# 24 attention items first in float32, then two token blocks per d_ff block

## Chip, cores, metric

One NeuronCore of a Trainium2 chip; all other cores are idle. The metric is the device time of one execution in microseconds (us), from the first to the last instruction and what lies around them.

## The reference

Sliding-window attention with a linear distance bias, then two MLPs on its output, all in float32:

```python
batch, n_heads, seq, head_dim = (4, 8, 576, 64);  n_tokens, d_model, d_ff = (2304, 512, 2048);  window = 128
...
    scores = scale * np.matmul(q, k.transpose(0, 1, 3, 2))
    mask = (rel >= 0) & (rel < window)
    scores = np.where(mask, scores + bias[None], -1000000000.0)
    scores = scores - np.max(scores, axis=-1, keepdims=True)
    attn = np.exp(scores)
    attn = attn / (np.sum(attn, axis=-1, keepdims=True) + 1e-09)
    return np.matmul(attn, v)
...
    h = x @ w_in;  g = np.maximum(h, 0.0) + alpha * np.minimum(h, 0.0);  x = g @ w_out         # first MLP
    h = x @ w_in2;  g = h * (1.0 / (1.0 + np.exp(-1.702 * h)));  out = g @ w_out2              # second MLP
```

The weights reach the kernel as 64-bit words and are turned into float32 on the chip.

## The kernel before, in words

**Attention items.** An item is one batch, one head and one unit of queries (`UNITS`: the first 256 queries, or the last 320). There are 64, in the order `u`, batch, head: 0 to 31 of the first unit, eight to a batch. An item runs through stages: load (`a_load`), scores on TensorE into a PSUM bank (`a_qk`), bias and row minimum on VectorE (`a_bias`, line 446), exponentials with row sums on ScalarE (`a_exp`, line 462), the sums plus 1e-9 and their reciprocal on VectorE (`a_recip`, lines 470 and 471), normalising on VectorE (`a_norm`, line 486), transposes on TensorE (`a_trans`, line 499), a copy of them to SBUF on ScalarE (`a_pt_hi`, line 506), the product with the values on TensorE (`a_av`), and for each pair of heads a high part and a rest of the result, on ScalarE and VectorE, into the ring `xh`/`xl` (`a_x3`, lines 572 and 573). The ring holds three blocks of 256 tokens.

**Two kinds of items.** The first `FP` = 16 are computed in float32: scores straight from the loaded rows (line 426, 64 rows), values placed into a zeroed tile by GpSimd (line 412), line 525 for the value product. All others are split into two float32r parts (`a_split`, lines 435, 436 and 537).

**Weights.** The first MLP has 32 chunks: for each d_ff block of 128 one of `w_in` and one of `w_out`, 512 KB each as it is loaded. A chunk is loaded (`w_load`, four buffers), then decoded: two operations on ScalarE (`w_scale`, lines 147 and 150), shift and add on VectorE (lines 154 and 159), and a split into a high part (line 107 on ScalarE; for chunks 0 and 2 line 108 on VectorE) and a rest (line 112 on VectorE). `w("...")` lets one chunk take one of these steps; while the list `pinned` isn't empty the decoding stays in its program order.

**Steps of the first MLP.** A step is one token block `k` and one d_ff block `f`: 12 matmuls for the hidden values (`m1_h`, line 586), a negated relu on ScalarE (line 600), the leaky combination on VectorE (line 606), its high part on ScalarE (line 608), the rest on VectorE, and two steps later (`LAG`) 12 matmuls into the block's accumulators (`m1_o`, line 632). After a block's last step ScalarE copies the accumulators and SP stores them (`x2d`, line 653). The steps run over all `f` of block 0, then all of block 1, then blocks 2 to 6 and a double block 7.

**Order.** Ten items (n = 0 to 9) are written out ahead of the steps, with decoding between their stages and idle matmuls (`busy`, counts in `WARM`) on TensorE. From item 10 on each step carries half an item (`item_a`: scores, transposes of the item ahead, bias, exponentials; `item_b`: value product, reciprocal, normalising), by the table `count` for the first 32 steps. At step 32 (`S2`) item 26 begins. In the first 32 steps each also moves one chunk on in its decoding, some of them two. Where nothing is pinned, the planner of the framework orders each engine's work by data dependences and its own estimate.

Of the kernel before, what the change touches and what calls it, by code (L numbers as in the profile page):

```python
# [43 lines left out]
HI_DVE = (0, 2)  # L44
NST, NWD = 4, 3
KM = NB1 - 2

FP = 16
# [6 lines left out]
WARM = (15, 3, 3, 2, 0, 1, 1, 1, 1, 1, 1)  # L55
# [14 lines left out]
def tile_window_attention__then__two_mlps(  # L70
# [248 lines left out]
    rawfs = [first.tile([P, UCOLS[0]], F32, name=f"rawf{i}") for i in range(2)]  # L319

    at = ExitStack()
    ps_a = at.enter_context(tc.tile_pool(name="ps_a", bufs=4, space=PSUM))
# [3 lines left out]
    sts = [ap_.tile([P, 16], F32, name=f"st{i}") for i in range(2)]  # L326
# [11 lines left out]
    pts = [apf.tile([P, 384], F32, name=f"pt{i}") for i in range(2)]  # L338
    zero = apf.tile([P, 512], BF16, name="zero")
# [79 lines left out]
    def a_qk(n, b, u, h, U):  # L419
        banks = [ps_a.tile([P, 2, 256], F32, tag="a", name="s") for _ in range(1 + u)]  # L420
# [20 lines left out]
    def a_bias(n, b, u, h, U):  # L441
        tt, s = tts[n % 2], sts[n % 2]
# [15 lines left out]
    def a_exp(n, b, u, h, U):  # L458
        tt, s = tts[n % 2], sts[n % 2]
# [7 lines left out]
    def a_recip(n, b, u, h, U):  # L467
        s = sts[n % 2]
# [4 lines left out]
    @stage  # L473
    def a_norm(n, b, u, h, U, eng):
        tt, s = tts[n % 2], sts[n % 2]
# [13 lines left out]
    def a_trans(n, b, u, h, U):  # L489
        tt = tts[n % 2]  # L490
        banks = [ps_a.tile([P, 512], F32, tag="a", name="pt") for _ in range(1 + u)]
# [10 lines left out]
    @stage  # L502
    def a_pt_hi(n, b, u, h, U, i):
        if i <= u:
            x, c, w = st["t", n][i]
            nc.scalar.copy(pts[n % 2] if n < FP else ar["pth"][:, c : c + w], x[:, :w])
# [13 lines left out]
    def a_av(n, b, u, h, U):  # L520
        if n < FP:
            x = st["x", n] = st["x", n - 1] if h % 2 else ps_a.tile([P, 512], F32, tag="a", name="x")
            pt, vz = pts[n % 2], vzs[n % 2]
# [7 lines left out]
        x = ps_a.tile([P, 512], F32, tag="a", name="x")  # L531
# [45 lines left out]
    gs, accs, part0 = {}, {}, []  # L577
# [39 lines left out]
    def m1_o(k, f):  # L617
# [4 lines left out]
        first = f == 0 or (k, f) == (0, 16)  # L622
        last = f == NF - 1 or (k, f) == (0, 16 - 1)
# [13 lines left out]
        if last:  # L637
            for i, a in enumerate(accs.pop(k)):
# [4 lines left out]
                if False:  # L643
                    pin(nc.vector.tensor_tensor(
                        xs, a, part0[0][:, i * DM : (i + 1) * DM].rearrange("p (i t) -> p i t", i=2), op=ALU.add
                    ))
                else:
                    copy("dve" if k == KM and i % 2 else "act", xs, a)
# [300 lines left out]
    idle = pso.tile([P, 2, T1], F32, tag="o1", name="idle")  # L949
# [4 lines left out]

    nc.vector.memset(zero, 0.0)
    for t in vzs:
# [3 lines left out]
    def w_first(n):  # L960
        for _ in range(n):
            i = wdone.get("load", 0)
            w_load(i)
            wdone["load"] = i + 1

    def bias_load(h, m):
        nc.sync.dma_start(out=relht[:, h : h + m, :], in_=relh[:, h : h + m, :])

    a_load(0, (0,))
# [8 lines left out]
    a_load(1, (1,))  # L978
    w_first(1)
    a_load(3, (0,))  # L980
    a_load(3, (1,))
    bias_load(4, 4)
    w_first(1)
    make_identity(nc, ident)
    busy(0)
    a_qk(0)
    w_ahead()
    def pre_load(n):
        if n + 4 < H + 2:
            a_load(n + 4)  # L990
        if n >= H:
            a_load(n + 2)

    def pre_qk(n):
        if n + 1 < H + 2:
            busy(n + 1)
            a_qk(n + 1)

    def pre_split(n):
        if n + 2 < H + 2:  # L1000
            a_split(n + 2)

    for n in range(H + 2):

        if n == 4:
# [4 lines left out]
            nc.gpsimd.tensor_scalar(beta, alph, -1.0, 1.0, op0=ALU.mult, op1=ALU.add)  # L1010
        a_av(n - 2)
        a_split_v(n)
        a_bias(n)
        w("split")
        a_exp(n)
        a_recip(n - 1)
        w("shift")
        a_norm(n - 1, "dve")
        a_trans(n - 1)
        w("add")  # L1020
        w_ahead()
        pre_load(n)
        a_x3(n - 2)
        a_pt_hi(n - 1, 0)
        a_pt_hi(n - 1, 1)
        pre_qk(n)
        w("scale")
        pre_split(n)
        if n in (0, 8, 9, 6, -1):
# [5 lines left out]
    n = H + 2  # L1035
    a_split(n)
    for i in range(2):
        a_pt_lo(n - 2, i)
    a_recip(n - 1)
    a_norm(n - 1, "dve")  # L1040
    a_av(n - 2)
    a_x1(n - 2)
    a_x2(n - 2)
    a_x3(n - 2)
# [4 lines left out]
    HF = 16  # L1049
    steps = [(0, f) for f in range(HF)] + [(1, f) for f in range(NF)] + [(0, f) for f in range(HF, NF)]  # L1050
# [3 lines left out]
    def item_a(n):  # L1054
        return (
            lambda: (a_trans(n - 1), a_qk(n), a_pt_hi(n - 1, 0)),
            lambda: (a_pt_hi(n - 1, 1), a_bias(n)),
            lambda: (a_pt_lo(n - 1, 0), a_pt_lo(n - 1, 1)),
# [4 lines left out]
    def item_b(n):  # L1063
        return (
            lambda: (
                a_av(n - 1), a_parts() if n == FP else None,
                a_recip(n), a_split_v(n), a_load(n + 2), a_norm(n, "dve"),
            ),
            lambda: a_x1(n - 1),
            lambda: a_x2(n - 1),  # L1070
            lambda: None,
            lambda: a_x3(n - 1),
# [3 lines left out]
    count = (1, 1, 1, 1, 1, 1, 1, 1, 1, 1, 1, 0, 1, 1, 2, 1, 1, 1, 1, 1, 1, 1, 1, 1, 1, 1, 1, 1, 2, 1, 1, 0)  # L1076
    halves, n = [], 2 * (H + 2)
    for c in count:
        halves.append([(item_a, item_b)[i % 2](i // 2) for i in range(n, n + c)])
        n += c  # L1080
    halves += [[(item_a, item_b)[i % 2](H + 2 + i // 2)] for i in range(S2, len(steps))]
    for s, (k, f) in enumerate(steps):
        n = H + 2 + s // 2
        if s == S2:
            pinned.clear()
        if (k, f) == (KM, 0):
            pinned.append(True)
        parts = halves[s]
        part = parts[0] if parts else NONE
        if len(parts) == 2:  # L1090
            m1_h(k, f)
            part[0]()
            part[1]()
            m1_n(k, f)
            m1_g(k, f)
            part[2]()
            part[3]()
            part[4]()
            w("shift")
            parts[1][0]()  # L1100
            parts[1][1]()
            w("add")
            w("scale")
            w_ahead()
            parts[1][2]()
            parts[1][3]()
            m1_lo(k, f, "dve")
            parts[1][4]()
# [279 lines left out]
```

## Time and profile before

| | us |
|---|---|
| median of 3 runs (lowest to highest) | 902.85 (900.74 to 903.24) |
| profiled execution, whole | 903.59 |
| its span, first to last instruction | 901.8 |
| TensorE busy | 885.6 (98%) |
| VectorE busy | 715.6 (79%) |
| ScalarE busy | 581.9 (65%) |
| GpSimd busy | 91.5 (10%) |

In the profile PE is TensorE, PEld its weight loads, DVE VectorE, ACT ScalarE, POOL GpSimd, SP the engine that issues the DMAs (SPq its queue). L586 is line 586 of the kernel. Matmuls are pipelined, and the duration of one includes a tail under which the next already runs: how long a row of matmuls takes is read from start to start. The same holds in a smaller measure for VectorE and ScalarE. A busy share is an average over stages with different limits.

### The profile page before, as it was taken

The page shows a single profiled execution, that of the slowest core. Times are in us where ns is not written, and L with a number is a line of the kernel's source. Part 1 is how long each engine was busy: PE and PEld are TensorE (multiplying, and loading weights), DVE is VectorE, ACT ScalarE, POOL GpSimd, SP SyncE. Part 2 cuts the span into 40 slices and gives each one's busy share as a digit, 9 for nine tenths or more (in the row PEclk, how much of TensorE's full clock was granted, in tenths as well). Part 3 has the DMA queues.
Part 4 walks back from the last instruction along what each step waited for, and adds up shares of the span by engine and source line. Part 5 has one row for each costly group of instructions (what it writes and reads, how often), then busy time and mean ns, then how long its engine had stood idle before and what let it go on. Part 6 is the DMA issues. An engine that isn't in the chain of part 4 may idle for free.

```text
span 901.8 us, 19339 instructions
## 1 busy us (share of the span) xinstructions
PE 885.6 (98%) x6882; PEld 848.9 (94%) x6884; DVE 715.6 (79%) x1906; ACT 581.9 (65%) x1459; POOL 91.5 (10%) x127
## 2 busy tenths in 40 slices
PE   7799999999999999999999999999999999999998
PEld 4589899999999999999988889999999999999998
DVE  5999877779989999999857777656665699989876
ACT  5999766767777778777645557655556755434332
POOL 1010111122222222222100000000000000000000
PEclk8989999999999999999999999999999999999999
DMA  8666521223424424235024324657668884544422
GB/s 256 213 210 210 166 80 48 83 81 99 163 87 124 132 87 143 84 89 163 19 72 139 94 74 162 206 190 242 237 237 286 286 288 141 164 139 119 141 71 95
DMA packets 73585, 133.43 MB, mean 148 GB/s; under 512 B 14224, under 2 KB 32656, under 8 KB 73488
## 3 DMA queue, kind: packets, MB, share of 16 engines
q1 hardware_dynamic: 73488, 132.19, 45.8%
q8 instruction: 54, 0.88, 0.4%
q14 instruction: 43, 0.35, 0.1%
HBM read 95.46 MB, written 36.70 MB: 147 GB/s over the span
## 4 chain that ended last, share of the span: by engine, by line
PE 94%; ACT 2%; DMA 1%; DVE 1%; issue 0%; SPq 0%; POOL 0%; ACTq 0%; DVEq 0%
PE h L586 22%; PE p L891 19%; PE o L632 17%; PE p L794 14%; PE h L794 6%; PE p L632 5%; PE x L537 3%; PE pt L499 3%; PE s L436 2%; PE s L435 2%; DMA raw<-in_u_dram 1%; PE s L426 1%; PE x L525 1%; ACT tt L462 0%; DVE wl L112 0%
## 5 line engine op out<-in xcount | busy, mean ns | idle before, releaser
L586 PE MATMUL h<-xh,wh 128*128 128x256 f32 (+1 forms) x512 | 152.1, 299 | 3.3 <-ACT xh L572 2.7
L586 PE MATMUL h<-xl,wh 128*128 128x256 f32 (+1 forms) x512 | 151.7, 297 | 0.5 <-DVE xl L112 0.5
L586 PE MATMUL h<-xh,wl 128*128 128x256 f32 (+1 forms) x512 | 151.4, 296 | 0.2 <-DVE wl L112 0.2
L891 PE MATMUL p<-wl,oh 128*128 128x256 f32 x504 | 136.2, 276 | 0.0
L891 PE MATMUL p<-wh,oh 128*128 128x256 f32 x504 | 135.0, 277 | 0.3 <-ACT oh L107 0.3
L891 PE MATMUL p<-wh,ol 128*128 128x256 f32 x504 | 131.0, 276 | 0.0
L632 PE MATMUL o<-gl,wh 128*128 128x256 f32 x448 | 124.7, 280 | 0.0
L632 PE MATMUL o<-gh,wl 128*128 128x256 f32 x448 | 124.0, 278 | 0.0
L632 PE MATMUL o<-gh,wh 128*128 128x256 f32 x448 | 123.5, 281 | 0.0
L586 PEld LDWEIGHTS h<-xh,wh 128*128 128x128 f32 x512 | 96.9, 190 | 7.8 <-ACT xh L572 4.0
L586 PEld LDWEIGHTS h<-xl,wh 128*128 128x128 f32 x512 | 97.3, 190 | 3.6 <-DVE xl L112 0.7
L586 PEld LDWEIGHTS h<-xh,wl 128*128 128x128 f32 x512 | 97.2, 190 | 3.3 <-DVE wl L112 0.4
L891 PEld LDWEIGHTS p<-wl,oh 128*128 128x128 f32 x504 | 94.6, 188 | 0.0
L891 PEld LDWEIGHTS p<-wh,oh 128*128 128x128 f32 x504 | 93.7, 188 | 0.5 <-ACT oh L107 0.5
L891 PEld LDWEIGHTS p<-wh,ol 128*128 128x128 f32 x504 | 91.4, 188 | 0.0
L632 PEld LDWEIGHTS o<-gl,wh 128*128 128x128 f32 x448 | 84.4, 188 | 0.1
L632 PEld LDWEIGHTS o<-gh,wl 128*128 128x128 f32 x448 | 84.4, 188 | 0.0
L632 PEld LDWEIGHTS o<-gh,wh 128*128 128x128 f32 x448 | 83.2, 188 | 0.8 <-issue 0.3
L600 ACT ACTIVATE n<-h 128x256 f32<-128x256 f32 (+1 forms) x128 | 51.7, 406 | 46.5 <-PE h L586 45.3
L462 ACT ACTIVATE tt<-tt,st 128x192 f32<-128x192 f32 (+2 forms) x160 | 74.6, 469 | 9.6 <-DVE st L446 9.6
L107 ACT CAST oh<-gs 128x1024 fp32r<-128x1024 f32 (+1 forms) x40 | 38.1, 964 | 62.9 <-issue 28.2
L794 PE MATMUL p<-xt,wh 128*128 128x288 f32 x320 | 64.6, 295 | 0.0
(154 smaller groups left out, 2372.0 us busy)
## 6 DMA issues: line engine op xcount, KB each, us to landing
g2d<-G SPq DMA_DIRECT2D x64, 288.0 KB, 3.0
ws<-in_w_in_dram SPq DMA_DIRECT2D x32, 512.0 KB, 3.7
ws<-in_w_out_dram SPq DMA_DIRECT2D x32, 512.0 KB, 4.7
gr<-g2d SPq DMA_DIRECT2D x32, 512.0 KB, 4.4
raw<-in_u_dram SPq DMA_DIRECT2D x32, 352.0 KB, 3.0
raw<-in_u_dram SPq DMA_DIRECT2D x16, 320.0 KB, 2.9
raw<-in_u_dram SPq DMA_DIRECT2D x32, 160.0 KB, 2.3
xr<-x2d SPq DMA_DIRECT2D x40, 128.0 KB, 2.6
```

The source lines that it names most:

```text
L107: return nc.scalar.copy(o, i)
L426: nc.tensor.matmul(o[:, :keys], raw[:, c0 : c0 + rows], raw[:, 256 + kk : 256 + kk + keys], start=True, stop=True)
L435: nc.tensor.matmul(o[:, :n_], q, kh[:, ks : ks + n_], start=True, stop=False)
L436: nc.tensor.matmul(o[:, :n_], q, kl[:, ks : ks + n_], start=False, stop=True)
L462: nc.scalar.activation(t, t, AF.Exp, bias=s[:rows, i : i + 1], scale=-1.0, accum_out=s[:rows, 4 + i : 5 + i])
L499: nc.tensor.transpose(banks[bank][:, dst : dst + P], src, ident)
L537: nc.tensor.matmul(x[:, oc : oc + nq], v, p[:, col : col + nq], start=(i == 0 and k == 0), stop=(i == len(js) - 1 and k == (j < 4)), skip_ ...
L586: nc.tensor.matmul(ph, w[:, 0, c * P : (c + 1) * P], x[:, c, r : r + n], start=(c == 0 and i == 0), stop=(c == NC - 1 and i == 2),)
L600: nc.scalar.activation(n, ph, AF.Relu, scale=-1.0)
L632: nc.tensor.matmul(o, w[:, 1, c * P : (c + 1) * P], g, start=(first and (k == KM or c % 2 == 0) and i == 0), stop=(last and i == 2), skip_ ...
L794: tc.keep_in_program_order(nc.tensor.matmul(o, w[:, cc * P : (cc + 1) * P], x[:, h, cc, i, :], start=first and cc == 0 and k == 0, stop=la ...
L891: mm = nc.tensor.matmul(o[:, m, :], g[:, a, m * P : (m + 1) * P], w, start=(p == 0 and m == 0 and i == 0), stop=(p == NF // 2 - 1 and i == 2),
```

## The change

`FP` grows from 16 to 24. All 24 float32 items are computed ahead of the steps, in a pipeline in which pass `n` handles the scores of item n + 1, bias and exponentials of n, normalising and transposes of n - 1, copy and value product of n - 2, and the split of n - 3; `chain` fixes the order of the pass on every engine. Three sets of work tiles are used in turn instead of two, and five load buffers instead of four. The score products run over 128 rows, with the lower 64 cleared to zero once. GpSimd adds the 1e-9. The value products go to the accumulator banks that are free at that time. Four weight chunks are loaded in passes 8 to 14, and decoding starts in pass 19 (`DEC`). Fewer idle matmuls are issued.

The first 32 steps then take blocks 0 and 1 in turn for each `f`; block 1 gets accumulators of its own out of the attention's PSUM banks. They carry one decoding move each and no items, but for the halves of items 24 and 25 in the last four; `held` places those behind the work of the step on each engine. From step 32 on the order of steps and items is as before. The high part of every chunk is made on ScalarE.

```diff
-HI_DVE = (0, 2)
+HI_DVE = ()
+DEC = (19, 21, 23, 24, 25, 26)
-FP = 16
+FP = 24
-WARM = (15, 3, 3, 2, 0, 1, 1, 1, 1, 1, 1)
+WARM = (9, 3, 3, 2, 1, 1, 1)
...
-    rawfs = [first.tile([P, UCOLS[0]], F32, name=f"rawf{i}") for i in range(2)]
+    rawfs = [first.tile([P, UCOLS[0]], F32, name=f"rawf{i}") for i in range(3)]
...
-    sts = [ap_.tile([P, 16], F32, name=f"st{i}") for i in range(2)]
+    sts = [ap_.tile([P, 16], F32, name=f"st{i}") for i in range(3)]
+    ttf = [first.tile([P, 512], F32, name="ttf")]
...
+    pts.append(first.tile([P, 384], F32, name="ptf"))
...
-        return (raws + rawfs)[n % 4] if n < H else raws[n % 2]
+        return (raws + rawfs)[n % 5] if n < FP else raws[n % 2]
...
+    def work_of(n):
+        i = n % 3 if n < FP else n % 2
+        return (tts + ttf)[i], sts[i]
...
-                raw = raw_of(n)[:D]
+                raw = raw_of(n)
...
-        nc.vector.tensor_scalar(s[:, 8 : 8 + m], s[:, 4 : 4 + m], 1e-9, None, op0=ALU.add)
+        if n >= FP:
+            nc.vector.tensor_scalar(s[:, 8 : 8 + m], s[:, 4 : 4 + m], 1e-9, None, op0=ALU.add)
         nc.vector.reciprocal(s[:, 12 : 12 + m], s[:, 8 : 8 + m])
...
+    def a_sum(n, b, u, h, U):
+        s = work_of(n)[1]
+        nc.gpsimd.tensor_scalar(s[:, 8:10], s[:, 4:6], 1e-9, None, op0=ALU.add)
...
-            x = st["x", n] = st["x", n - 1] if h % 2 else ps_a.tile([P, 512], F32, tag="a", name="x")
-            pt, vz = pts[n % 2], vzs[n % 2]
+            if h % 2:
+                x = st["x", n] = st["x", n - 1]
+            else:
+                i = n // 2 % 2
+                x = pso.tile([P, 2, T1], F32, tag=f"o{i}", name=f"o{i}").rearrange("p i t -> p (i t)")
+                st["x", n] = x
+            pt, vz = pts[n % 3], vzs[n % 2]
...
+    def a_xf(n, b, u, h, U, part):
+        if h % 2:
+            r = b * T1 % RING
+            hi, x = xh[:, h // 2, r : r + T1], st["x", n][:, :T1]
+            if part:
+                sub("dve", xl[:, h // 2, r : r + T1], x, hi)
+            else:
+                copy("act", hi, x)
...
-                accs[k] = [pso.tile([P, 2, T1], F32, tag=f"o{i}", name=f"o{i}") for i in range(2)]
+                pool = psa["j"] if k == 1 else pso
+                accs[k] = [pool.tile([P, 2, T1], F32, tag=f"o{i}", name=f"o{i}") for i in range(2)]
...
+    nc.vector.memset(raws[0][D:, :512], 0.0)
+    nc.vector.memset(raws[1][D:, :512], 0.0)
+    for t in rawfs:
+        nc.gpsimd.memset(t[D:, :512], 0.0)
...
     a_load(0, (0,))
-    w_first(1)
-    w_first(1)
-    bias_load(0, 2)
-    a_load(2, (1,))
+    bias_load(0, 1)
     a_load(1, (0,))
     a_load(0, (1,))
     a_load(2, (0,))
+    bias_load(1, 1)
+    a_load(1, (1,))
+    a_load(3, (0,))
     bias_load(2, 2)
...
+    for n in range(-1, FP + 3):
+        only(a_qk, n + 1)
+        busy(n + 2)
+        only(a_bias, n)
+        only(a_xf, n - 3, 0)
+        only(a_pt_hi, n - 2, 0)
+        only(a_av, n - 2)
+        only(a_recip, n - 1)
+        only(a_norm, n - 1, "dve")
+        only(a_trans, n - 1)
+        only(a_xf, n - 3, 1)
+        only(a_exp, n)
+        only(a_split_v, n - 1)
+        only(a_sum, n)
+        if n == 0:
+            a_load(4, (1,))
+        elif 0 < n < FP - 4:
+            a_load(n + 4)
+        elif FP - 4 < n < FP - 1:
+            a_load(n + 3)
+        if n in (8, 10, 12, 14):
+            w_load(wdone.setdefault("load", 0))
+            wdone["load"] += 1
...
+        if n in DEC:
             w("split")
             w("shift")
             w("add")
             w_ahead()
             w("scale")
+    chain(mark)
...
+    psa["j"] = pj.enter_context(tc.tile_pool(name="ps_j", bufs=1, space=PSUM))
+    psa["a"] = pj.enter_context(tc.tile_pool(name="ps_b", bufs=2, space=PSUM))
...
-    steps = [(0, f) for f in range(HF)] + [(1, f) for f in range(NF)] + [(0, f) for f in range(HF, NF)]
+    steps = [(k, f) for f in range(NF) for k in range(2)]
...
+    def item_half(s):
+        n, i = divmod(s - S2, 2)
+        return (item_a, item_b)[i](n + FP + 2) if s >= S2 - 4 else NONE
...
+        part = item_half(s)
+        if s == S2 - 6:
+            held(lambda: a_split(FP))
+        if s < S2:
+            part = [lambda f=f: held(f) for f in part]
...
+        if s == S2 + 2:
+            pj.close()
+            psa["a"] = at.enter_context(tc.tile_pool(name="ps_c", bufs=4, space=PSUM))
```

## Rows read from the trace of the kernel before

**Rows 1.** The page's chain of work that ended last: share by engine

```profile
PE 94%; ACT 2%; DMA 1%; DVE 1%; issue 0%; SPq 0%; POOL 0%; ACTq 0%; DVEq 0%
```

**Rows 2.** Windows: stretch, length, busy us (instructions) per engine, clock, DMA share, GB/s

```profile
45.00:112.20 67.20, 65.56 (x479) 60.10 (x480) 60.02 (x169) 58.99 (x150) 7.51 (x13) 0.95 0.63 197
112.20:167.20 55.00, 55.00 (x478) 55.00 (x478) 41.15 (x141) 36.98 (x121) 10.82 (x18) 1.00 0.21 65
```

**Rows 3.** Timeline of SP: start, us, engine, line, operation; stores of blocks 0, 1

```profile
112.81 0.81 SPq L653 DMA_DIRECT2D x2d<-xs  x2
...
167.84 1.19 SPq L653 DMA_DIRECT2D x2d<-xs  x2
```

**Rows 4.** The chain in order of time, 180 to 200 us: start, us, what

```profile
188.65 1.36 PE h L586 x12
190.01 0.33 PE pt L499 x3
...
190.79 1.38 PE o L632 x12
```

**Rows 5.** Timeline of TensorE: scores (L426) and value products (L525) of items

```profile
12.66 1.65 PE L426 MATMUL s<-rawf 64*128 64x128 f32 x4
...
20.05 0.89 PE L525 MATMUL x<-pt,vz 128*128 128x256 f32 x4 [0.23 <-ACT pt L506]
20.78 0.27 PE L499 MATMUL pt<-ident,tt 128*128 128x128 f32 x1
20.98 0.92 PE L426 MATMUL s<-raw 64*128 64x128 f32 x4
21.83 0.44 PE L499 MATMUL pt<-ident,tt 128*128 128x128 f32 x2
```

**Rows 6.** Windows of 2 us, TensorE alone: busy (instructions), granted clock, DMA share, GB/s

```profile
42.00:44.00 2.00, 0.92 (x5) 1.00 0.88 315
...
46.00:48.00 2.00, 2.00 (x8) 0.50 0.78 238
```

**Rows 7.** Timeline of ScalarE, 40 to 44 us: an item and a chunk

```profile
40.70 0.48 ACT L506 COPY pt<-pt 128x384 f32<-128x384 f32 x1
41.08 0.67 ACT L147 ACTIVATE wd<-ws 128x512 f32<-128x512 f32 x1
...
42.73 0.41 ACT L462 ACTIVATE tt<-tt,st 128x128 f32<-128x128 f32 x1
...
43.61 0.36 ACT L572 CAST xh<-x 128x256 fp32r<-128x256 f32 x1
```

**Rows 8.** Timeline of VectorE, 40.5 to 45 us

```profile
40.69 0.16 DVE L471 RECIPROCAL st<-st 128x2 f32<-128x2 f32 x1
...
41.30 0.69 DVE L112 TENSOR_TENSOR wl<-wd,wh 128x512 fp32r<-128x512 f32 x1
41.91 0.54 DVE L486 TENSOR_SCALAR tt<-tt,st 128x128 f32<-128x128 f32 x2
...
43.47 0.42 DVE L154 TENSOR_SCALAR wd<-wd 128x512 int32<-128x512 int32 x1
...
43.93 0.69 DVE L159 CUSTOM_DVE_ANT_0 wd<-ws,wd 128x1024 uint16<-128x1024 uint16 x1
44.54 0.42 DVE L112 TENSOR_TENSOR xl<-x,xh 128x256 fp32r<-128x256 f32 x1
```

**Rows 9.** Timelines of TensorE and VectorE, the start

```profile
1.19 5.27 PE L953 MATMUL idle<-zero 128*128 128x512 bf16 x15 [1.19 <-DVE zero L955]
...
8.51 0.29 DVE L446 CUSTOM_DVE_ANT_0 tt<-s,relht 128x128 f32<-128x128 f32 x1 [7.38 <-DMA relht<-in_relh_dram]
```

**Rows 10.** GpSimd: the small add (timeline); value copies of line 412, ns min/median/max

```profile
22.11 0.20 POOL L1010 TENSOR_SCALAR beta<-alph 128x16 f32<-128x16 f32 x1 [4.06 <-DMA alph<-in_alpha_dram]
...
L412 POOL COPY vz<-raw x12: 289/294/1096, 9.2 to 91.1; 128x128 f32<-128x128 f32 x12
```

**Rows 11.** DMA issues, 45 to 90 us: count, KB each, median us to landing

```profile
ws<-in_w_in_dram SPq DMA_DIRECT2D x9, 512.0 KB, 4.4
```

More of the change, by code (lines that the diff above doesn't have):

```diff
@@ L419, in a_qk @@
     def a_qk(n, b, u, h, U):
-        banks = [ps_a.tile([P, 2, 256], F32, tag="a", name="s") for _ in range(1 + u)]
+        banks = [psa["a"].tile([P, 2, 256], F32, tag="a", name="s") for _ in range(1 + u)]
         places = []
@@ L489, in a_trans @@
     def a_trans(n, b, u, h, U):
-        tt = tts[n % 2]
-        banks = [ps_a.tile([P, 512], F32, tag="a", name="pt") for _ in range(1 + u)]
+        tt = work_of(n)[0]
+        banks = [psa["a"].tile([P, 512], F32, tag="a", name="pt") for _ in range(1 + u)]
         for i, (c0, rows, kk, keys) in enumerate(U["chunks"]):
@@ L621, in m1_o @@
         hi, lo = wt[0, f]
-        first = f == 0 or (k, f) == (0, 16)
-        last = f == NF - 1 or (k, f) == (0, 16 - 1)
+        first, last = f == 0, f == NF - 1
         if first:
@@ L642, in m1_o @@
                     xs = xsp[0].tile([P, 2, T1], F32, tag="xs", name="xs")
[L643 to L648, printed above, removed]
+                copy("dve" if k == KM and i % 2 else "act", xs, a)
                 if k == KM:
@@ L953, in busy, with chain, held @@
             tc.keep_in_program_order(nc.tensor.matmul(idle, zero[:, :P], zero, start=True, stop=True))
+    def chain(mark):
+        last, on = {}, False
+        for i in list(tc.nc.cur_bb.bb.instructions):
+            if on:
+                if i.engine in last:
+                    tc.add_manual_dep(
+                        i, last[i.engine].name,
+                        mybir.DependencyInfo(mybir.DependencyClass.NoSync, mybir.DependencyReason.DATA),
+                        reason="chain",
+                    )
+                last[i.engine] = i
+            on = on or i is mark
+    def held(fn):
+        last, done = {}, set()
+        for i in tc.nc.cur_bb.bb.instructions:
+            last[i.engine] = i
+        mark = i
+        fn()
+        on = False
+        for i in list(tc.nc.cur_bb.bb.instructions):
+            if on and i.engine not in done:
+                done.add(i.engine)
+                tc.add_manual_dep(
+                    i, last[i.engine].name,
+                    mybir.DependencyInfo(mybir.DependencyClass.NoSync, mybir.DependencyReason.DATA), reason="held",
+                )
+            on = on or i is mark
     nc.vector.memset(zero, 0.0)
+    nc.vector.memset(raws[0][D:, :512], 0.0)
+    nc.vector.memset(raws[1][D:, :512], 0.0)
+    for t in rawfs:
+        nc.gpsimd.memset(t[D:, :512], 0.0)
     for t in vzs:
@@ L959, in tile_window_attention__then__two_mlps @@
         nc.gpsimd.memset(t, 1.0)
[L960 to L964, printed above, removed]
     def bias_load(h, m):
         nc.sync.dma_start(out=relht[:, h : h + m, :], in_=relh[:, h : h + m, :])
+    block = tc.nc.cur_bb.bb
+    mark = block.instructions[-1]
     a_load(0, (0,))
-    w_first(1)
-    w_first(1)
-    bias_load(0, 2)
-    a_load(2, (1,))
+    bias_load(0, 1)
     a_load(1, (0,))
@@ L1034, in tile_window_attention__then__two_mlps @@
             w("scale")
[L1035 to L1044, printed above, removed]
-    at0.close()
+    chain(mark)
+    nc.gpsimd.tensor_scalar(beta, alph, -1.0, 1.0, op0=ALU.mult, op1=ALU.add)
+    at0.close()
+    pa.close()
+    a_parts()
+    pj = ExitStack()
+    psa["j"] = pj.enter_context(tc.tile_pool(name="ps_j", bufs=1, space=PSUM))
+    psa["a"] = pj.enter_context(tc.tile_pool(name="ps_b", bufs=2, space=PSUM))
     gp[0] = p1.enter_context(tc.tile_pool(name="g", bufs=3, side="right"))
@@ L1089, in tile_window_attention__then__two_mlps @@
[L1089 to L1098, printed above, removed]
+        m1_h(k, f)
+        part[0]()
+        if s < S2:
+            w_ahead()
+        m1_n(k, f)
+        if s < S2:
             w("shift")
-            parts[1][0]()
-            parts[1][1]()
+        m1_g(k, f)
+        part[1]()
+        part[2]()
@@ L1102, in tile_window_attention__then__two_mlps @@
+        if s < S2:
             w("add")
[L1103 to L1108, printed above, removed]
-            w("split")
-        elif s < S2:
-            m1_h(k, f)
-            part[0]()
-            w_ahead()
-            m1_n(k, f)
-            w("shift")
-            m1_g(k, f)
-            part[1]()
-            part[2]()
-            w("add")
-            part[3]()
-            m1_lo(k, f, "dve")
+        part[3]()
@@ L1122, in tile_window_attention__then__two_mlps @@
+        m1_lo(k, f, "dve")
+        if s < S2:
             w("split")
             w("scale")
[L1124 to L1140 removed]
@@ L1141, in tile_window_attention__then__two_mlps @@
[L1141 to L1143 removed]
+        part[4]()
         if 2 <= k < 6 or k == 6 and f < 4:
```

115 lines of the change are left out of this document (28 added, 87 removed).

## The prediction

> **What bounds the kernel now.** I read the chain of waits first: TensorE holds 94% of it [rows 1], so a change pays only where it takes work or waiting off TensorE. "Busy" hides where it waits, because the view counts overlapping tails; so I counted its instructions by stretch [rows 2]. From 112.2 to 167.2 us it starts 478 matmuls in 55.0 us, or 8.7 per us; from 45.0 to 112.2 it starts 479 in 67.2 us, or 7.1 per us, and in that first stretch VectorE and ScalarE are each busy for 59 to 60 of 67.2 us. There both weight decoding and attention sit on those two engines, and TensorE waits. After that TensorE is the bound and stays so to the end. What can be won lies before about 112 us.
>
> The change leaves the order of the work alone from step 34 on: steps s >= 32 run the same token blocks, with the same item halves (26 at step 32), before and after. So I compare one moment: the end of step 33, which before is when the second pair of block results is stored. The pair of block 0 is stored at 112.8, that of block 1 at 167.8 [rows 3]. The moment before is 167.8 us; later work shifts with it.
>
> A pure step is 12 matmuls of line 586 and 12 of line 632, and 12 of either take 1.36 us when TensorE is dense [rows 4]: 2.72 us. The 16 steps between the two stores took 55.0 us, 3.44 each, with 16 item halves in them: 0.72 us for a half.
>
> **The change part by part.**
>
> *32 steps with almost no items.* Steps 0 to 33 hold 34 groups of line 586 and 32 of line 632 (the second runs two steps late): 66 x 1.36 = 89.8 us. Only six item halves are left in them (steps 28 to 33): 6 x 0.72 = 4.3. Together 94.1 us. So the change breaks even if the attention ahead of it ends at 167.8 - 94.1 = 73.7 us.
>
> That needs the decoding not to take over. Each step decodes one chunk. On ScalarE it takes 0.67, 0.68 and 0.62 by durations, but 42.73 - 41.08 = 1.65 us from start to start [rows 7]; with the step's two operations on 256 columns (0.36 each by the nearest row of that size) 2.4 us. On VectorE: shift 0.42, add and split 0.61 each from start to start (41.30 to 41.91, 43.93 to 44.54), two operations on 256 columns 0.42 each: 2.5 us [rows 8]. Both fit into 2.72 us, at 88 and 91%; [rows 2] shows 88 and 89% of a whole stretch, so there is little to spare. Loads: 512 KB in 2.72 us is 193 GB/s against 197 GB/s moved on average in the first stretch of [rows 2]; a chunk lands in 4.4 us [rows 11] and is loaded about two steps, 5.4 us, ahead. I cost these at nothing, hidden behind TensorE; if that cover is gone, see rival 4.
>
> *24 float32 items in a pipeline.* One pass costs TensorE one score product, one value product and three transposes. At full clock the scores on 64 rows take 0.92 by duration (0.85 to the next start, 20.98 to 21.83), the value product on 128 rows 0.89 (0.73 to the next start, 20.05 to 20.78) [rows 5]. Three transposes took 0.33 when dense [rows 4], one alone 0.20, so 0.33 to 0.60; I take 0.47. With the scores now on 128 rows at the value product's 0.73, a pass is 1.93; as waits for the copy of the transposes leave small holes (0.23 at 20.05) I take 2.05, bounds 1.75 and 2.4.
>
> The scores and the value product have the same number of columns in the two matmuls, and the rows differ by 0.12 us in favour of 128 rows. The Trainium skill (TensorE: Matmul & The Clock Gate, "Step-by-step: what each phase is for") says that loading weights goes by columns and that the row count doesn't matter. By it the half of zeros would buy nothing and a pass would be 0.12 us longer, some 2.5 us in all; the rows here speak for a gain.
>
> The other engines have less in a pass. ScalarE: copy 0.38, exponentials 0.88, half of a 0.36 copy: 1.4 us [rows 7]. VectorE: reciprocal and bias 0.61 (40.69 to 41.30), normalising 0.54, half of a 0.42 subtraction: 1.4 [rows 8]. The round trip of one item (copy, exponentials, sum on GpSimd, reciprocal, normalising, transposes) spans two passes. The sum has no row: the nearest is a tensor_scalar of 16 columns, 0.20; the upper bound is the 128-column copy, 0.29 to 1.10 [rows 10]; I take 0.25, because it is the same operation. That gives 0.38 + 0.88 + 0.25 + 0.16 + 0.54 + 0.47, and 0.2 for waits, = 2.9 us for two passes, 1.45 per pass, or 1.9 with the sum at 1.10: under 2.05 either way.
>
> *The start.* 15 warm-ups took 5.27 us, and the first bias waited to 8.51 for its table, behind two weight loads [rows 9]. Nine warm-ups end at 4.4 by that mean; I take 5.0. The table is now second in SP's queue and no weight load stands before it. From the first scores at 5.0: scores 0.9, bias 0.6, exponentials 1.0, sum 0.3, reciprocal and normalising 0.7, transposes 0.5, waits 0.4: the pass in which all stages run begins at about 9.4. The memory clears (VectorE, GpSimd) run beside the warm-ups: nothing. If the loads are late, up to 1.5 us.
>
> *The passes.* 21 passes x 2.05 = 43.1: the last scores end at 52.5. Decoding in passes 19, 21 and 23 adds 1.1 or 1.65 to ScalarE's 1.4 [rows 7], past 2.05 by 0.45, 0.45 and 1.0: 1.5 in all (bounds 0 and 2): 54.0.
>
> *The drain.* From the last scores to the last value product: bias 0.6, exponentials 1.0, sum 0.3, reciprocal and normalising 0.7, transposes 0.5, copy 0.5, value product 0.7, waits 0.5, and about 1.9 of decoding that is queued ahead of those on ScalarE and VectorE: 6.7 us. TensorE has 3.2 us of item work in it; one of the first two 1.36 us groups of step 0 and 1 should fit into the hole (bounds none, both): 5.4 us. Attention's end, as TensorE's time counts it: 59.4.
>
> *Waits added.* "held" only orders the six item halves behind each step; queued behind them is the same step's weight work, and no row shows it late. The banks of the second accumulator change hands at step 34 after ScalarE's copies: 0 to 1 us, I take 0.5. Loads: five buffers, issued three passes (6 us) ahead, against 4.4 us for 512 KB [rows 11]: nothing. SP's queue is passed by four early weight loads only.
>
> *Sum.* 59.4 + 94.1 + 0.5 = 154.0 against 167.8: 13.8 us less. The profiled execution took 903.59 (span 901.80): 889.8. The median of the three runs is 0.7 lower: 889.
>
> **The rivals.**
>
> 1. *The clock falls once or twice.* Before, TensorE was busy for 0.92 of the 2 us from 42 on, and from 46 to 48 the granted clock is 0.50, which is 1.2 GHz [rows 6]; at that level the scores took 1.65 rather than 0.92 [rows 5]. The fill and the drain are the two thin places after the change. Some 7 us at the lower level cost 3.5: 892.5 to 896. For: the drain is half empty. Against: warm-ups and hoisted groups fill it.
>
> 2. *Passes of 1.75,* if transposes run at their dense 0.33 and no hole is left: 21 x 0.3 = 6.3 less: 883.
>
> 3. *The round trip paces the passes at 2.4,* by semaphores and by GpSimd's sum meeting VectorE. 21 x 0.35 = 7.4 more: 896. For: the 1.10 us copies [rows 10]. The Trainium skill (GPSIMD Engine Reference, "1. Specifications") says that GpSimd shares its SBUF interfaces with VectorE; the long copies agree.
>
> 4. *The steps are paced by decoding, not by TensorE.* ScalarE and VectorE would be as full as in the first stretch of [rows 2], and the loads at 98% of its rate. At 3.1 us a step for 28 steps: 10.6 more: 900; from 3.2 us on nothing is won.
>
> 5. *Slower: the float32 passes run at 1.2 GHz throughout.* By 1.65 against 0.92 [rows 5] a pass of 1.93 becomes about 3.5: 21 x 1.45 = 30 more: 919. It decides from the tenth such pass on. Against: the passes fill TensorE nearly wholly, and the same products in looser order ran at full rate at 20 us [rows 5].
>
> **How the numbers follow.** Forecast (885 to 893) 0.48, rival 1 0.19, rival 2 0.10, rival 3 0.11, rival 4 0.06, rival 5 0.06. The range takes the forecast and rivals 1 to 3: 882 to 899, and leaves out most of 4 and 5 and the edge of 2. About 0.3%, 2.7 us, is what a measurement of this kernel can tell from no change: faster is below 900.1, the first four cases (0.88, less a little for the tail of 3, 0.87); same is half of rival 4 and that tail (0.05); slower the rest (0.08).
>
> **What would show it.** In the profile after: line 525 or its like recurring every 2.0 to 2.1 us with full clock; the last value product near 58 to 60 us; line 586 and 632 in pieces of 12 at 1.36 us up to step 28; the first store of block results and the second only a step apart, the second near 154 us; the rest unchanged and TensorE dense. The prediction is wrong if TensorE waits in the passes for ScalarE, VectorE or a load, if the clock row shows more than one stretch at 0.50, or if steps are longer than 2.8 us.

## The result, and the profile after

The changed kernel takes 893.0 us (median; 892.1 to 896.2) against 902.2 for the kernel before (900.7 to 903.2): a ratio of 0.9905, 95% interval 0.9876 to 0.9934. That is 9.2 us less. Forecast was 889, with a range of 882 to 899. The direction and the range held; the point lay 4 us too low.

The granted clock fell at one thin place of the changed program in one profiled execution and not in another, and these two differ by about 3 us; where that matters, the text says which one is meant. The one shown first took 896.15 us, span 894.4.

The chain of work that ended last, share by engine, after ([rows 1] has 94%):

```profile
PE 97%; ACT 1%; DVE 1%; issue 0%; POOL 0%; ACTq 0%; DVEq 0%; POOLq 0%
```

Stretches of the changed kernel, with the columns of [rows 2] (TensorE, its weight loads, VectorE, ScalarE, GpSimd, each busy us and instructions; granted clock, DMA share, GB/s): passes, drain, and the steps in two parts.

```profile
10.00:45.00 35.00, 34.13 (x203) 26.40 (x201) 26.78 (x136) 28.29 (x101) 9.25 (x37) 1.00 0.65 178
45.00:68.00 23.00, 17.88 (x103) 15.81 (x104) 18.29 (x54) 19.95 (x53) 3.71 (x11) 0.85 0.48 151
68.00:112.20 44.20, 44.20 (x378) 44.20 (x377) 38.62 (x80) 36.35 (x79) 0.00 (x0) 1.00 0.65 200
112.20:157.60 45.40, 45.40 (x389) 45.40 (x388) 36.43 (x91) 33.31 (x87) 3.68 (x6) 1.00 0.46 138
```

From 68 to 112.2 TensorE now starts 8.6 matmuls per us, where [rows 2] has 7.1 up to 112.2. VectorE and ScalarE are busy for 87 and 82% and no longer set the pace.

The stores of the block results, answering [rows 3]:

```profile
154.03 4.63 SPq L677 DMA_DIRECT2D x2d<-xs  x3
...
159.25 0.42 SPq L677 DMA_DIRECT2D x2d<-xs  x1
```

**The passes.** TensorE's timeline of one pass (start, us, line, operation; compare [rows 5]):

```profile
17.11 0.82 PE L434 MATMUL s<-rawf 128*128 128x128 f32 x4
17.98 0.89 PE L544 MATMUL o<-pt,vz 128*128 128x256 f32 x4
18.71 0.49 PE L513 MATMUL pt<-ident,ttf 128*128 128x128 f32 x3
19.04 0.82 PE L434 MATMUL s<-rawf 128*128 128x128 f32 x4
19.92 0.89 PE L544 MATMUL o<-ptf,vz 128*128 128x256 f32 x4
```

The value product (line 544) recurs after 19.92 - 17.98 = 1.94 us: scores 0.87 to the next start, value product 0.73, transposes 0.33. No idle time stands in brackets: TensorE paces these passes. The first three full passes take 1.88 each, and one late pass has a hole, the first row below.

**The drain.** The rows of the same timeline with idle time ahead of them, and what ended it. The last scores start at 48.76, so the first of these rows still belongs to the passes:

```profile
45.77 0.89 PE L544 MATMUL o<-pt,vz 128*128 128x256 f32 x4 [0.78 <-ACT pt L520]
...
50.37 0.89 PE L544 MATMUL o<-ptf,vz 128*128 128x256 f32 x4 [0.79 <-ACT ptf L520]
...
52.30 0.89 PE L544 MATMUL o<-pt,vz 128*128 128x256 f32 x4 [0.72 <-ACT pt L520]
...
58.52 0.89 PE L544 MATMUL o<-ptf,vz 128*128 128x256 f32 x4 [0.66 <-ACT ptf L520]
...
61.46 0.58 PE L615 MATMUL h<-xh,wh 128*128 128x256 f32 x1 [2.05 <-DVE g L635]
```

Behind the last value product TensorE stands for 2.05 us until VectorE's line 635 frees a bank of hidden values. The chain leads back from there to ScalarE, which decodes a chunk before it comes to the first relu (line 629):

```profile
58.27 0.62 ACT wh L108
58.89 0.58 ACT wd L148
...
60.29 0.29 ACT n L629
```

In this execution the granted clock falls there (windows of 2 us, TensorE alone: busy, instructions, clock, DMA):

```profile
60.00:62.00 2.00, 0.54 (x2) 0.67 0.46 168
62.00:64.00 2.00, 2.00 (x12) 0.50 0.78 264
```

The chain of the same stretch (start, us, what) shows the price: 24 matmuls behind the hole take 5.49 us instead of two groups of 1.36, 2.8 us more. And it shows something else: from 70 on a group of 12 takes 1.41, not the 1.36 of [rows 4].

```profile
61.46 5.49 PE h L615 x24
66.95 3.13 PE o L661 x24
70.08 1.41 PE h L615 x12
71.49 1.41 PE o L661 x12
```

**Where the rest went.** The first matmul of step 34 marks the forecast's "end of step 33". Before, and then after:

```profile
167.84 0.28 PE L586 MATMUL h<-xh,wh 128*128 128x256 f32 x1
```

```profile
157.65 0.28 PE L615 MATMUL h<-xh,wh 128*128 128x256 f32 x1
```

That is 10.2 us earlier. From there to the end of the span the kernel before needs 901.8 - 167.84 = 734.0 us, the changed one 894.4 - 157.65 = 736.7, for the same work in the same order: 2.7 us are lost *behind* the change. One window holds them; TensorE is busy throughout and the clock is 1.00, but it starts 25 matmuls fewer. Before, and then after:

```profile
220.00:430.00 210.00, 210.00 (x1838) 1.00 0.39 120
```

```profile
220.00:430.00 210.00, 210.00 (x1813) 210.00 (x1812) 188.16 (x606) 158.46 (x465) 51.59 (x53) 1.00 0.37 112
```

25 x 0.115 us is 2.9 us. So two things were open: what the hole and the clock cost, and why matmuls at full clock start further apart.

### The profile page after: what moved, and what is told of

It reads as the page before. It is cut to its first block, busy times and chain, and to the rows that moved or that the text cites. A ratio compares the mean times of both kernels' runs of the same rounds, so it can differ in the third digit from the quotient of the medians.

```text
span 894.4 us, 19342 instructions
## 1 busy us (share of the span) xinstructions
PE 882.7 (99%) x6876; PEld 852.1 (95%) x6876; DVE 706.1 (79%) x1858; ACT 575.7 (64%) x1429; POOL 89.5 (10%) x147
## 4 chain that ended last, share of the span: by engine, by line
PE 97%; ACT 1%; DVE 1%; issue 0%; POOL 0%; ACTq 0%; DVEq 0%; POOLq 0%
PE h L615 23%; PE p L915 19%; PE o L661 18%; PE p L818 14%; PE h L818 6%; PE p L661 5%; PE pt L513 3%; PE x L556 3%; PE o L544 2%; PE s L434 2%; PE s L444 1%; PE s L443 1%; PE idle L977 1%; ACT wh L108 0%; ACT wd L148 0%
## 5 line engine op out<-in xcount | busy, mean ns | idle before, releaser
L470 ACT ACTIVATE tt<-tt,st 128x256 f32<-128x256 f32 (+1 forms) x144 | 67.5, 471 | 7.4 <-DVE st L454 7.4
L635 DVE SCALAR_TENSOR_TENSOR g<-n,beta,h 128x256 f32<-128x256 f32 x112 | 53.3, 477 | 18.4 <-ACT n L629 16.9
```

Of the source, the lines that this page charges most:

```text
L470: nc.scalar.activation(t, t, AF.Exp, bias=s[:rows, i : i + 1], scale=-1.0, accum_out=s[:rows, 4 + i : 5 + i])
L635: nc.vector.scalar_tensor_tensor(g, n, beta[:, f : f + 1], ph, op0=ALU.mult, op1=ALU.add)
```

## The experiments

**The changed kernel again.** No edit.

> The changed kernel once more, beside the kernels below on the same chip. My theory (TensorE is the bound in passes and steps; the rest of the forecast gain went to a 2.05 us hole at 59.4 us and the lower clock until 66.6 us, 2.8 us, and to matmuls that start 118 ns apart instead of 113): about 893 us, the hole again, the lower clock again, and the distance of the matmuls free to differ from execution to execution. Rival (the distance is set by what the steps do beside TensorE): 118 ns in steps 2 to 33 in every profile.

892.95 us, ratio 0.9891 [0.9876, 0.9905]; span 891.1. The hole is there with 2.05 us, but the clock stays up behind it (rows of the windows and of the chain):

```profile
60.00:62.00 2.00, 1.08 (x9) 1.00 0.56 143
...
60.92 3.09 PE h L615 x24
...
66.84 1.41 PE h L615 x12
```

Step 34 begins at 154.41, 0.4 us behind the forecast's 154.0. The rest takes 891.1 - 154.41 = 736.7 again, with 1813 matmuls from 220 to 430, and groups in the steps take 1.41 again. So the slower starts don't need the clock's fall: both profiles of this kernel have them, one with the fall and one without.

**The hole filled with idle matmuls.**

```diff
+    warm = psa["a"].tile([P, 512], F32, tag="a", name="warm")
+    for _ in range(8):
+        nc.tensor.matmul(warm, zero[:, :P], zero, start=True, stop=True)
     chain(mark)
```

> Eight idle matmuls behind the last value product, in the hole between 59.4 and 61.5 us. My theory: the wait for VectorE stays, the clock doesn't fall, the 24 matmuls of line 615 behind the hole take 2.7 to 2.8 us instead of 5.5, and the kernel is 2.8 us faster than the changed one, about 890. Rival (ScalarE and VectorE with their decoding pace the first steps, so that TensorE would wait for them instead): the clock stays up, but waits of 2 to 3 us appear in the steps up to 80 us and the time stays at 893.

891.42 us, 0.9878 [0.9864, 0.9892]; the interval overlaps that of the run before. The hole shrinks to 0.32 us, the clock stays at 1.00, and the groups in the steps are at 1.36:

```profile
61.77 3.01 PE h L615 x24
...
67.50 1.36 PE h L615 x12
```

From 220 to 430 there are still 1813 matmuls. The work behind the hole starts no earlier (61.77 against 60.92); what differs between the two profiles is the pitch in the steps. The mean granted clock is 1.000 in all four executions here and 0.995 to 1.000 in the five of the run before, which fits a fall that no longer comes.

**One idle matmul instead of eight.** The same edit with `range(1)`.

> One idle matmul behind the last value product instead of eight. In the run with eight the clock had no need to be saved (it hadn't fallen in the run of the changed kernel beside it either), and yet the matmuls of the steps up to 137 us started 113 ns apart and not 118. Theory A (the hole in TensorE's work sets the distance): with one idle matmul the hole stays at about 1.8 us and the steps run at 118 ns (groups of 12 in 1.41 us): about 893. Theory B (the kind of instruction that stands ahead of the dense stretch sets it): one is enough, groups of 12 take 1.36 us from 62 to 137 us: about 891.5.

891.88 us, 0.9888 [0.9870, 0.9907]. The hole is 1.83 us, nearly as long as before, and yet the groups behind it take 1.36 up to about 133 us. So it isn't a filled hole that decides between 1.36 and 1.41 there; the next run, with the full 2.05 us, says the same. Nor is it the idle matmul alone: several of the runs below have 1.36 without one. Again 1813 from 220 to 430.

```profile
60.85 3.01 PE h L615 x24
...
66.58 1.36 PE h L615 x12
```

**No idle matmuls at the start.**

```diff
-WARM = (9, 3, 3, 2, 1, 1, 1)
+WARM = ()
```

> All idle matmuls left out, at the start and in the first passes. My theory: TensorE starts at the lower clock and raises it only some microseconds into the passes; passes at 1.2 GHz take about 3.4 us instead of 1.94, so two to four of them cost 3 to 6 us: 896 to 899. Rival 5 of the prediction (float32 passes alone don't raise the clock at all): all passes at 3.4 us, 920 or more. Third: the passes start 1 us earlier and nothing is lost: 892.

892.18 us, 0.9887 [0.9870, 0.9904]: nothing changes in the time. The first scores start at 3.67 us and run at the lower rate for a while (the first eight matmuls 2.90 us), but passes of 1.88 and then 1.93 follow from 9 us on. Behind the hole, again of 2.05 us, the clock falls in this execution (0.50 from 60 to 66 us), and the steps' groups take 1.36. So a fallen clock and slow starts are independent both ways.

```profile
60.40 5.49 PE h L615 x24
...
68.91 1.36 PE h L615 x12
```

**Decoding early in the passes.**

```diff
-DEC = (19, 21, 23, 24, 25, 26)
+DEC = (6, 9, 12, 15, 18, 21)
-        if n in (8, 10, 12, 14):
+        if n in (2, 4, 5, 7):
```

> Decoding of the first chunks spread over passes 6, 9, 12, 15, 18 and 21 instead of 19 to 26, loads of the first four chunks moved up to passes 2 to 7. My theory: ScalarE has 0.5 us to spare in a pass, so a chunk of 1.65 us in every third pass costs at most 0.2 us there; the drain loses the 1.9 us of decoding ahead of its copies and the hole gets shorter, so attention's end comes 2 to 4 us earlier and the clock may stay up: 887 to 891. Rival (the drain is a chain of waits that decoding hardly lengthens; the stalls move into the passes): 892 to 895.

900.61 us, 0.9978 [0.9959, 0.9998], spread from 896.4 to 907.5 in twelve executions: the gain is nearly gone. This was meant to empty the drain, and it broke the passes instead. With the weight loads moved up, an item's rows came late, and TensorE waited:

```profile
30.73 1.62 PE L434 MATMUL s<-rawf 128*128 128x128 f32 x4 [2.19 <-DMA rawf<-in_u_dram]
...
69.24 0.38 PE L615 MATMUL h<-xh,wh 128*128 128x256 f32 x1 [1.86 <-DVE g L635]
```

The scores behind that wait take 1.62 rather than 0.82, the lower rate. The hole before the steps is still there. As loads and decoding moved together, it doesn't say what the drain alone costs; the next run leaves the first four loads where they are.

**Decoding one or two passes earlier.**

```diff
-DEC = (19, 21, 23, 24, 25, 26)
+DEC = (17, 19, 21, 23, 24, 25)
```

> Decoding in passes 17, 19, 21, 23, 24 and 25 instead of 19, 21, 23, 24, 25 and 26; loads unchanged. My theory of the hole (ScalarE and VectorE are in the decoding of pass 26 when the first step's relu could run): the hole behind the last value product shrinks from 2.05 us by about the 1.65 us of that chunk, passes are delayed by at most 0.4 us, and the kernel is about 1.3 us faster than the changed one, 891 to 892. Rival (as in the run with early decoding, the decoding only moves the stalls into the passes): 893 or above.

895.74 us, 0.9928 [0.9914, 0.9942]: 2.8 us slower than the changed kernel run again. The stalls didn't go away; they moved to the last passes and grew:

```profile
57.59 0.89 PE L544 MATMUL o<-pt,vz 128*128 128x256 f32 x4 [1.93 <-ACT pt L520]
59.78 1.62 PE L544 MATMUL o<-ptf,vz 128*128 128x256 f32 x4 [0.97 <-ACT ptf L520]
63.88 0.58 PE L615 MATMUL h<-xh,wh 128*128 128x256 f32 x1 [2.49 <-DVE g L635]
```

In each of the three placements tried the copy of the transposes waits on ScalarE behind decoding, and here the clock falls earlier: the value product at 59.78 takes 1.62. The steps start 3.0 us later than in the changed kernel run again (63.88 against 60.92). Their groups take 1.36 here, with no idle matmul added, so the whole time shows less than the attention lost.

**The steps block after block.** The new attention, but the steps over block 0 first and then block 1, with a second decoding move in 14 of them.

```diff
-    steps = [(k, f) for f in range(NF) for k in range(2)]
+    steps = [(k, f) for k in range(2) for f in range(NF)]
...
         part[4]()
+        if s < 14:
+            w("shift")
+            w("add")
+            w_ahead()
+            w("split")
+            w("scale")
```

> One part of the change undone: all of block 0, then all of block 1, as before, so that each of the first 14 steps decodes two chunks; the 24 float32 items stay ahead. My theory: two chunks cost ScalarE 3.3 us and, with the step's own work, 4 us against 2.7 us on TensorE, so the first 14 steps are paced by decoding and the kernel is 16 to 20 us slower than the changed one: 909 to 913, slower than before. Rival (the gain comes from taking the items out of the first steps, and the interleaving of the two blocks is worth little): 893 to 898.

911.32 us, 1.0097 [1.0081, 1.0113]: slower than before. The same stretch, 80 to 120 us, in this kernel and then in the changed one run again:

```profile
80.00:120.00 40.00, 33.17 (x233) 30.96 (x234) 37.13 (x76) 36.55 (x74) 0.00 (x0) 0.91 0.79 250
```

```profile
80.00:120.00 40.00, 40.00 (x342) 40.00 (x341) 35.48 (x74) 33.30 (x73) 0.00 (x0) 1.00 0.65 193
```

VectorE and ScalarE do the same 73 to 76 instructions in 40 us, so decoding goes at its own pace, but 109 fewer matmuls lie beside it. With the rest of the change in place, sharing each decoded chunk between two blocks is worth 18 us between these two kernels; part of that is the clock, 0.91 against 1.00 here. The other way round, the blocks in turn without the new attention, wasn't tried.

**Scores on 64 rows.**

```diff
-                raw = raw_of(n)
+                raw = raw_of(n)[:D]
```

> One part undone: score products over 64 rows again. My theory: a score product takes 0.85 us instead of 0.66 to 0.73 from start to start, TensorE is the bound of a pass, and a pass becomes 0.12 to 0.2 us longer: 23 passes, 3 to 4.5 us slower than the changed kernel, 896 to 897.5. Rival (the row count doesn't matter for loading weights, and the low 0.66 comes from the denser order): 893.

898.94 us, 0.9959 [0.9926, 0.9992], but this median lies in a gap: five of the ten executions took 893.5 to 896.1, the other five 901.8 to 907.9. The profiled execution (901.78 us), one of the second five, shows two things. A pass takes 34.04 - 32.01 = 2.03 us:

```profile
31.16 0.92 PE L434 MATMUL s<-rawf 64*128 64x128 f32 x4
32.01 0.92 PE L544 MATMUL o<-pt,vz 128*128 128x256 f32 x4
32.77 0.49 PE L513 MATMUL pt<-ident,tt 128*128 128x128 f32 x3
33.19 0.92 PE L434 MATMUL s<-raw 64*128 64x128 f32 x4
34.04 0.92 PE L544 MATMUL o<-pt,vz 128*128 128x256 f32 x4
```

And up to 24 us the products run at the lower rate (value product 1.49, scores 1.65), although the column of the granted clock shows 1.00. Here a window of this kernel, and then the same of the changed kernel:

```profile
16.00:24.00 8.00, 8.00 (x25) 1.00 0.14 37
```

```profile
16.00:24.00 8.00, 7.72 (x45) 1.00 0.51 136
```

25 instructions in 8 us against 45 are 3.6 us lost in these 8 alone. So the half of zeros buys 0.09 us a pass, 1.9 in 21. Whether it also brings the full rate early isn't shown: no profile was kept of the faster five. The whole times understate the loss, too, as the steps' groups take 1.36 in this profile and 1.41 in the changed kernel's.

**The 1e-9 on VectorE.**

```diff
-        if n >= FP:
-            nc.vector.tensor_scalar(s[:, 8 : 8 + m], ...
+        nc.vector.tensor_scalar(s[:, 8 : 8 + m], ...
...
-        only(a_sum, n)
```

> The changed kernel with the 1e-9 of the float32 items added on VectorE again (0.17 us each before) instead of on GpSimd. Theory of the forecast: TensorE paces the passes, VectorE has room for 0.17 in a pass of 1.94, so nothing: 892.3 to 893.5, value products still 1.94 apart. Rival: the way over GpSimd (0.21 and its two waits) is in what paces the pass; then passes come some 0.1 shorter and the kernel 2 us faster. Other rival: VectorE becomes late in the passes that decode, up to 0.17 in each of six: 893.5 to 894.5.

893.73 us, 0.9905 [0.9885, 0.9926]: no difference from the changed kernel that can be measured. Passes are still 21.99 - 20.06 = 1.93 us:

```profile
20.06 0.89 PE L544 MATMUL o<-ptf,vz 128*128 128x256 f32 x4
21.99 0.89 PE L544 MATMUL o<-pt,vz 128*128 128x256 f32 x4
```

**The place of 64 bytes.** The changed kernel allots a third small tile for minima and sums, 16 numbers or 64 bytes per partition, ahead of `tb`, `ident`, `relt`, `xp`, `q`, `kh`, `kl` and the later items' transposed tiles and values. This moves all of those by 64 bytes. The edit puts it where the memory is given back after the float32 items; the order of the work stays. It also moves `ttf` and `ptf`, which only the passes use.

```diff
-    sts = [ap_.tile([P, 16], F32, name=f"st{i}") for i in range(3)]
+    sts = [ap_.tile([P, 16], F32, name=f"st{i}") for i in range(2)]
+    sts.append(first.tile([P, 16], F32, name="stf"))
```

> The changed kernel with one thing moved: the third of the small tiles for minima and sums (64 bytes in each partition) lies in the memory that is given back after the float32 items, so that everything behind it (q, kh, kl, the transposed tiles of the later items) lies where it lay before the change. The order of the work is the same. Disputed is why the matmuls of lines 615 and 661 start 118 to 120 ns apart from 200 to 435 us, where before they started 115 to 118 ns apart. Theory A, the place in memory: these windows go back to 115 to 118 and the kernel gets 2 to 3 us faster, 890.0 to 891.0. Theory B, the order of instructions ahead: the same rows as in the changed kernel, 892.3 to 893.4.

889.41 us, 0.9851 [0.9829, 0.9874]. That lies just below the interval of the changed kernel run again (0.9874 against 0.9876). The window from 220 to 430 has the 1838 matmuls of the kernel before again:

```profile
220.00:430.00 210.00, 210.00 (x1838) 1.00 0.36 108
```

and the chain's groups there take 1.36; this kernel first, then the changed one:

```profile
69.98 1.36 PE h L616 x12
...
309.52 1.36 PE o L662 x12
```

```profile
309.60 1.41 PE o L661 x12
```

From the first matmul of step 34 (154.74; the clock had fallen in this execution, with the 24 matmuls at 5.49 again) to the end it takes 888.4 - 154.74 = 733.7 us, as before. So the place in memory decides the late part, by 64 bytes. The profiles leave no overlap: with the place of before (the kernel before, this one, and the last run below) that part takes 733.7 to 734.1 us with 1838 matmuls in the window; with the changed kernel's place, in its two profiles and those of its nine other variants, 736.3 to 737.6 us with 1813 to 1815.

The groups of the steps are at 1.36 too, but there the place isn't needed for it, as the runs above show. Nor do the whole times fit one pitch per kernel: three executions of this kernel at a mean clock of 1.00 took 886.56, 886.57 and 889.91 us. That difference of 3 us is about what the pitch in the steps is worth (the 96.2 us of steps 0 to 33 in the changed kernel run again are 151.05 - 60.41 + 2 x 1.36 = 93.4 in the next run, both without a fall). Whether that pitch changes between executions isn't shown, as those were not profiled.

**One idle matmul behind the passes and none at the start,** the two edits above together.

> The changed kernel without idle matmuls at its start (as in the run without them), and with one idle matmul behind the last pass. Without the idle ones at the start the last value product came about 1 us earlier (57.5) and the steps' matmuls started 113 ns apart up to 131 us, but the granted clock fell behind the hole of 2.05 us. If one idle matmul shortens the hole to 1.8 as it did there, and the clock stays: 890.0 to 891.0. If the clock falls all the same: 892 to 893.

890.71 us, 0.9885 [0.9862, 0.9909]: not to be told from the changed kernel run again. Hole 1.84 us, clock 1.00, groups in the steps at 1.36, 1814 matmuls from 220 to 430.

**All three together.**

> The changed kernel with the third small tile in the memory that is given back (as in the run on the place), one idle matmul behind the last pass and no idle matmuls at the start. The place alone gave matmuls 113 ns apart in the steps and the 1838 matmuls of before between 220 and 430 us instead of 1813; the other two gave 113 ns in the steps up to 131 us, an attention that ends about 1 us earlier and, with the one idle matmul, a granted clock that stayed up behind the hole in two profiled executions of two. If these add up where they don't overlap: 1838 matmuls again and 887 to 888. If the cadence comes of an accident of the order that the place and the idle matmul only happen to hit, 1813 again and 889.5 to 891.5.

886.57 us, 0.9847 [0.9825, 0.9868]; span 884.7. Step 34 begins at 150.65, the rest takes 734.1 us:

```profile
220.00:430.00 210.00, 210.00 (x1838) 1.00 0.35 105
```

It is the fastest of the kernels run, though its interval overlaps that of the place alone.

## Why the prediction came out as it did

The sum against the changed kernel run again, whose clock stayed up (us):

| | forecast | measured | off by |
|---|---|---|---|
| attention's end, as TensorE's time counts it | 59.4 | 58.2 (60.92 - 2 x 1.36) | -1.2 |
| steps 0 to 33 with halves and handover | 94.6 | 96.2 (154.41 - 58.2) | +1.6 |
| from step 34 to the end of the span | 734.0 | 736.7 | +2.7 |
| whole, with 1.8 around the span | 889.8 | 892.95 | +3.1 |

**The step that failed is "later work shifts with it".** The forecast argued that the order of the work is the same from step 34 on, and it is. But it took "same order" for "same time". The work came 2.7 us dearer because the change also moved tiles in memory: the diff shows `range(2)` become `range(3)` in `sts`, and that line was costed at nothing. Moving the 64 bytes back gave 733.7 and 734.1 us for that part, in two kernels. The kernel itself gave a hint: it holds fillers (`padk`, the pads of `shift`) that do nothing but place tiles.

**Passes: right, for partly other reasons.** Forecast 2.05 with a floor of 1.93; measured 1.94, with one hole, of 0.78 at 45.77, where the forecast had 1.5 us for decoding. TensorE waiting for ScalarE in a pass was one of its signs of being wrong, and this one wait is such a sign. The scores on 128 rows did not come down to the value product's 0.73, they took 0.87 to the next start; the transposes took 0.33 rather than 0.47. The first scores of a full pass start at 9.54 (forecast 9.4). The zeros' gain, 0.12 a pass by [rows 5], is 0.09 by the run on 64 rows: 1.9 us rather than 2.5. It sits in the transposes (0.42 against 0.33) and the value product (0.76 against 0.73) that follow, not in the scores' own pitch (0.85 against 0.87). The Trainium skill (TensorE: Matmul & The Clock Gate, "Step-by-step: what each phase is for") lets the row count make no difference to a weight load; the scores' pitch by itself agrees, the pass as a whole doesn't.

**Passes and drain: two errors that cancel.** The last scores were forecast to end at 54.0; in the first profile they start at 48.76 and end near 49.6, 4.4 us earlier. Of these, 1.2 is a count: from the first scores of a full pass to the end of the last there are 20 passes and one score product, not 21 passes. The rest is shorter passes and less waiting in them. In exchange the drain is longer: from 49.6 to 61.46, 11.9 us, 2.7 of them both first groups of line 615. That leaves 9.2 against a forecast of 5.4. Decoding was costed as 1.5 us in the passes; most of its stalls (0.79, 0.72 and 0.66 us, and the hole of 2.05) fall into the drain, where ScalarE's queue holds it ahead of the copies and of the first relu. With decoding one or two passes earlier they grew (1.93, 0.97 and 2.49).

**Steps: right in kind.** The forecast had 1.36 per group and 4.8 us for six halves and the handover. In the kernel with all three edits, 150.65 - 60.06 = 90.6 us less 64 groups of 1.36 leaves 3.5 for these. In both profiles of the changed kernel groups take 1.41 instead, which makes up for that and more; why they do in the steps stays open. Decoding is hidden, as costed: 87 and 82% against the 91 and 88% forecast, and TensorE is busy for all of 68 to 157.6 us.

**The rivals.** *The clock falls* (892.5 to 896) is what the first profile shows: 2.8 us at the drain, 896.15. It didn't happen in the profile run again at 892.95, so the distance from 889 comes about without it. Whether it happened in the unprofiled executions isn't shown. *Passes of 1.75* didn't come: the transposes ran at 0.33 and all passes but one had no hole, as that needed, but the scores took 0.87. *The round trip paces the passes*: no; the sum on GpSimd took 0.21 us (forecast 0.25), taking it away moved nothing, and GpSimd's copies of 128 columns stayed at 0.29 where [rows 10] has up to 1.10. *Steps paced by decoding*: no in the change, yes as soon as the blocks are not interleaved (911). *Passes at 1.2 GHz* (919): not in the changed kernel, but with 64 rows the passes of the first 24 us of one profiled execution ran at the lower rate.

## What to carry to other kernels

When two engines that prepare operands pace the one that consumes them, use each prepared operand twice before preparing the next: here that was worth 18 us beside the rest of the change, and without it the rest made the kernel slower than before. A part of the program that "only shifts" must be compared by its own length, before and after; if it grew, count instructions per stretch at equal clock, and look at which tiles the change moved in memory. Work taken out of one tight stretch of a queue comes back in the next one, so price it where it lands.

## What the runs showed of the hardware

- Dense matmuls of 256 columns at a granted clock of 1.00 come in two pitches, 12 in 1.36 or in 1.41 us. From step 34 on the place of some tiles decides: a shift by 64 bytes changed the pitch over 210 us (1838 against 1813 to 1815 matmuls, without overlap over 14 profiles). Which of the moved tiles matters, and why, stays open; it wasn't tried.
- In steps 0 to 33 it is open what decides. Groups took 1.41 in both profiles of the changed kernel, with early decoding and with the 1e-9 on VectorE; 1.36 with any edit of the idle matmuls, with the place, with 64 rows and with decoding one or two passes earlier. Times of executions of one kernel at nearly the same clock differ by as much as this pitch is worth, so it may not belong to the program.
- The same hole of 2.05 us ahead of the steps was followed by a fallen clock in some profiled executions (the first of the changed kernel, the one without idle matmuls, the one with the place alone) and not in others (the changed kernel again, the scores on 64 rows, the 1e-9 on VectorE, all three edits). With holes of 1.83 and 1.84 us it stayed up both times. The fall costs 2.8 us.
- The column of the granted clock does not show everything: in the run on 64 rows it stands at 1.00 from 16 to 24 us, while scores took 1.65 us there and 0.92 from 25 us on.
